# Narrow-tile matmul runs merged and placed side by side, with half of the weighted-value products written over V

## The chip, the cores and the metric

One core of a Trainium2 chip runs the kernel. The metric is the device time of one execution in microseconds (us). "Span" is the time from the first to the last instruction in a profile; it is some 1.7 us shorter than the timed figure in the same execution.

## The reference

```python
xn = _layernorm(x)                       # x: 1 x 2048 x 512, bf16
# A: attention, 32 heads of 16, each row looks at W = 8 rows, 2 apart, backwards
q, k, v = split(xn @ wqkv)
idx = pos[:, None] - arange(8) * 2       # negative ones masked
logits = einsum("bhsd,bhswd->bhsw", q, k[idx]) * Dh ** -0.5
o = einsum("bhsw,bhswd->bhsd", softmax(logits), v[idx])
# B: gated feed-forward, 1376 wide
h = gelu(xn @ w_gate) * (xn @ w_up)
return x + o @ wo + h @ w_down
```

## The kernel before

The rows are worked on in four blocks of 512 (0 to 3). Almost all matmuls are 128 columns of weights by 512 columns of data: Q, K, V (L1130), gate and up (L1367), the output sums (L1442, L1446). Attention over 8 neighbours is not a matmul, so Vector (DVE) multiplies Q by shifted K (the logit products, 8 per block), and TensorE only adds up groups of rows, with weights of ones and zeros. These sums use the array as four tiles of 32 columns side by side (`tile_position`), four matmuls abreast. A "visit" below is an unbroken run of matmuls in narrow tiles between full-width ones; a "slot" is the time from one matmul's start to the next (0.216 us for 512 columns, or for four such matmuls abreast). The small `u10` piece (the last 64 columns of gate and up) uses tiles of 64 and is issued with the logit sum:

```python
for kt in range(4):                       # u10: two 64-column tiles
    for c in range(2):
        e.matmul(PS[64 * c:64 * c + 64, ...], lhsT=Wt[:, kt, 128:192], rhs=xnT[..., 256 * c:256 * c + 256],
                 start=(kt == 0), stop=(kt == 3), tile_position=(0, 64 * c))
for (g, prs) in grp:                      # logit sum: 32 matmuls, 32-column tiles
    for wq in range(2):
        for sj in range(4):
            e.matmul(PS[32 * sj:32 * sj + 32, ...], lhsT=E8[:, ...],
                     rhs=UNI[:, prs[wq].slot, :, sj * 128:(sj + 1) * 128], ..., tile_position=(0, 32 * sj))
```

The weighted-value sum works in the same way on the products of V and the softmax. V comes back from device memory with shifts into four buffers `BS`; Vector multiplies each twice (half 0 and 1), and both products go to one of twelve buffers `UNI`, shared with the logit products:

```python
e.tensor_tensor(out=bass.AP(UNI, ito.slot * 2048, ...), in0=bass.AP(BS, ...), in1=bass.AP(PT, ...), op=ALU.mult)
...
for (dq_, itp, it) in grp:                # PVR_MERGE = 2 of them: 16 matmuls
    for half in range(2):
        for d4 in range(4):
            e.matmul(PS[32 * d4:32 * d4 + 32, ...], lhsT=E4[:, :], rhs=UNI[:, itp[half].slot, d4, :],
                     start=(half == 0), stop=(half == 1), tile_position=(0, 32 * d4))
```

The order on each engine is made at build time by a planner in the kernel: each piece of work is a task with a priority (shifted by a table `SHIFT`), reads and writes of buffers from pools with quotas, and a mode ("c" for the narrow tiles, "f" for full width).

Of the kernel before, what the change touches and what calls it, by code (L numbers as in the profile page):

```python
# [11 lines left out]
    TOL=dict(pe=0.6, act=-0.3, dve=0.0, pool=0.0, sp=0.0),  # L12
    DMA_ISSUE=0.48,
    DMA_FIXED=2.0,
    DMA_BPUS=330e3,
    ACT_SWITCH=1.35,
    PE_SLACK=0.0,
# [128 lines left out]
class Graph:  # L146
# [118 lines left out]
    def schedule(self, params=None, prior=None):  # L265
# [4 lines left out]
        TOL = prm["TOL"]  # L270
        DMA_ISSUE = prm["DMA_ISSUE"]
        DMA_FIXED = prm["DMA_FIXED"]
        DMA_BPUS = prm["DMA_BPUS"]
        ACT_SWITCH = prm["ACT_SWITCH"]
        PE_SLACK = prm["PE_SLACK"]
# [3 lines left out]
        pe_mode = [None]  # L279
# [78 lines left out]
        while nsched < ntot:  # L358
# [43 lines left out]
            for e, cl in cands.items():  # L402
                tol = TOL[e]
                cur = list(cl)
                if prior is not None and use_virtual[0]:
                    pmin = min(c[1].prio for c in cl)
                    real = set(c[1].idx for c in cl)
                    hor = efree[e] + 6.0
                    for t in unsched[e]:
                        if t.start is None and t.idx not in real and t.prio < pmin and t.latest is None:  # L410
                            ps = prior.get(t.idx)
                            if ps is not None and ps < hor:
                                cur.append((max(ps, efree[e]), t, 0.0, ps, True))
                while True:
                    top = min(cur, key=lambda c: (c[1].prio, c[1].idx))
                    lim = top[3] + tol
                    nxt = [c for c in cur if c is not top and
                           c[0] + c[2] + (DMA_ISSUE if e == "sp" else c[1].dur) <=
                           (lim if c[1].latest is None else top[3])]
                    if not nxt:  # L420
                        break
                    cur = nxt
                pick = top
                if pick[4]:
                    blocked.append(e)
                    continue
                if best is None or (pick[0], pick[1].idx) < (best[0], best[1].idx):
                    best = pick
# [6 lines left out]
            for it in t.items:  # L435
                if it.pool is not None and it.slot is None:
                    pool = it.pool
# [175 lines left out]
    def report(self):  # L613
# [11 lines left out]


SHIFT = {
    "acc0": 91, "acc2": 150, "acc3": 165, "er0": -90, "er3": -43, "ffn0": -489, "ffn1": 431, "ffn2": 3,
    "ffn3": 355, "fin2": -301, "fin3": -17, "h1": -471, "h2": -1698, "ldb2": 617, "ln1": -107, "ln2": -2,
    "ln3": -224, "prod1": 434, "prod2": -302, "prod3": -2237, "pv1": 744, "pv3": -110, "pvr0": -321,  # L630
    "pvr1": -1104, "pvr2": -106, "pvr3": 108, "qkv2": 179, "qkv3": -756, "sm2": 1187, "sm3": 124,
}
SCHED = dict(PE_SLACK=1.0, DMA_BPUS=250e3,
             TOL=dict(pe=0.3, act=-0.3, dve=-0.3, pool=-0.3, sp=0.0))

GROUPS = ((r"(?:bnst|bnag|ve|sq|rstd|sub|norm)(\d+)$", "ln", 4), (r"trx(\d+)", "ln", 2),
          (r"(?:mm|evq|evk|evv|stv)(\d)_", "qkv", 1), (r"pr(\d)_", "prod", 1), (r"er(\d)_", "er", 1),
# [21 lines left out]
def d_dve(n, rate=1.04):  # L659
    return 0.07 + n * rate * 1e-3  # L660
# [6 lines left out]
def bass_parallel_sum__sliding_local_dilated__glu_gated_geglu__prompt_kernel(nc, A_x, A_wqkv, A_wo, B_x, B_w_gate, B_w_up, B_w_down, out, dbg=None, cfg=None):  # L667
    cfg = dict(cfg or {})
# [5 lines left out]
    NUNI = cfg.get("NUNI", 12)  # L674
# [7 lines left out]
    NBS = cfg.get("NBS", 4)  # L682
# [3 lines left out]
    NXR = cfg.get("NXR", 2)  # L686
    NOB = cfg.get("NOB", 3)
    NDMASEM = cfg.get("NDMASEM", 24)
    QUOTAS = cfg.get("QUOTAS", dict(tp=2, qkv=2, lg=2, o=cfg.get("PVR_MERGE", 2), ffn=3,
                                    acc=2))  # L690
    PB_ = cfg.get("PRIO_BLOCK", 1000)
    LN_BASE = cfg.get("LN_BASE", [-30, 10, 1010, 2010])
# [1 line left out]
    R_WG = cfg.get("R_WG", -800)  # L694
    TAIL_SPLIT = {14: [(0, 256), (256, 512)], 15: [(0, 256), (256, 384), (384, 512)]}
    NHALF = cfg.get("NHALF", [1, 1, 1, 1])
    PVR_MERGE = cfg.get("PVR_MERGE", 2)
    CHAIN_SHIFT = cfg.get("CHAIN_SHIFT", [0, 300, 600, 900])
    FFN_BASE = cfg.get("FFN_BASE", 500)
    FFN_STEP = cfg.get("FFN_STEP", 1000)  # L700
# [8 lines left out]
    with contextlib.ExitStack() as es:  # L709
# [57 lines left out]
        P_qt = Pool("qt", NQT)  # L767
        P_kt = Pool("kt", 2)
        KTI = [Item("kt%d" % b, P_kt, "k") for b in range(4)]
        P_uni = Pool("uni", NUNI, quotas=cfg.get("UNI_Q", dict(p=8, pv=8)))  # L770
        P_ms = Pool("ms", NMS)
        P_pb = Pool("pb", NPB)
        P_pt = Pool("pt", NPT)
# [283 lines left out]
        for b in range(NB):  # L1057
# [7 lines left out]
            if b == 0:  # L1065
                lead = []
                for t in range(4):
                    for which in range(2):
# [15 lines left out]
                               + ([(XTI[0], ("y", 0, t))] if t < 2 else []))  # L1084
                        gs = (0, 1, 2, 3)
                        if t == 0 and which == 0:
                            t_mm = G.task("pe", "mma0_0", 12 * 0.0563, mk_mm((0, 1, 2)), rd=mrd, wr=[it_mm],
                                          prio=-100, mode="f")
                            t_mm.urgent = True
                            t_of["mma0_0"] = t_mm  # L1090
                            gs = (3,)
                        t_mm = G.task("pe", "mmt%d_%d" % (which, t), 4 * len(gs) * 0.0563, mk_mm(gs), rd=mrd,
                                      wr=[it_mm], prio=-100 + t, mode="f")
                        t_mm.urgent = True
# [82 lines left out]
            for g in range(4):  # L1177
                prs = []
                for wq in range(2):
                    it_pr = pr_items[g][wq]  # L1180
                    prs.append(it_pr)

                    def mk_p(wq=wq, g=g, it=it_pr, itq=it_qt, itk=KTI[b]):
                        return lambda e: e.tensor_tensor(  # L1184
                            out=UNI[:, it.slot, :, :],
                            in0=bass.AP(QT, (itq.slot * 4 + g) * 512, [[NQT * 4 * 512, 128], [0, 4], [1, 512]]),
                            in1=bass.AP(KT, (itk.slot * 4 + g) * 528 + 4 - 2 * wq, [[2 * 4 * 528, 128], [4, 4], [1, 512]]),
                            op=ALU.mult)
                    rdk = ([(KTI[0], ("t", t)) for t in range(4)] if b == 0 else [(KTI[b], g)]) + [(KTI[b], "pad")]
                    rdq = [(it_qt, ("t", t)) for t in range(4)] if b == 0 else [(it_qt, (g, 0))]  # L1190
                    G.task("dve", "pr%d_%d_%d" % (b, wq, g), d_dve(2048, 0.52), mk_p(),
                           rd=rdq + rdk, wr=[(it_pr, "d")] + ([(q, "a") for gg in range(g, g + ER_MERGE) for q in pr_items[gg]
                                                      if q is not it_pr] if g % ER_MERGE == 0 and wq == 0 else []),
                           prio=base + 20)
# [96 lines left out]
                   prio=base + 37, nbytes=256 * 1024)  # L1291

            it_ot = Item("ot%d" % b, P_ot, "ot")
            pv_items = [[Item("pv%d_%d_%d" % (b, dq, half), P_uni, "pv") for half in range(2)] for dq in range(4)]
            pvr_grp = []
            for dq in range(4):
                it_bs = Item("bs%d_%d" % (b, dq), P_bs, "bs")
                for j in (0, 2, 1, 3):
                    def mk_l(j=j, dq=dq, it=it_bs, c0b=c0b):
                        return lambda e: e.dma_start(  # L1300
# [11 lines left out]
                for half in range(2):  # L1312
                    def mk_pv(half=half, it=it_bs, ito=it_pv[half], itp=it_pt):
                        o = 2 - 2 * half
                        return lambda e: e.tensor_tensor(  # L1315
                            out=bass.AP(UNI, ito.slot * 2048,
                                        [[NUNI * 2048, 128], [512, 4], [128, 4], [1, 128]]),
                            in0=bass.AP(BS, it.slot * 4 * 514 + o,
                                        [[NBS * 4 * 514, 128], [514, 4], [128, 4], [1, 128]]),
                            in1=bass.AP(PT, itp.slot * 1024 + half * 128,  # L1320
                                        [[NPT * 1024, 128], [0, 4], [256, 4], [1, 128]]),
                            op=ALU.mult)
                    G.task("dve", "pv%d_%d_%d" % (b, dq, half), d_dve(2048, 0.52), mk_pv(),
                           rd=[it_bs, it_pt], wr=[(it_pv[half], "d")] + ([(q, "a") for dd in range(dq, dq + PVR_MERGE) for q in pv_items[dd]
                                                      if q is not it_pv[half]]
                                                     if dq % PVR_MERGE == 0 and half == 0 else []), prio=base + 50)
                it_o = Item("o%d_%d" % (b, dq), P_ps, "o")
                pvr_grp.append((dq, it_pv, it_o))
                if len(pvr_grp) == PVR_MERGE:
                    def mk_pr(grp=list(pvr_grp)):  # L1330
                        def f(e):
                            ins = None
                            for (dq_, itp, it) in grp:
                                for half in range(2):
                                    for d4 in range(4):
                                        ins = e.matmul(PS[32 * d4:32 * d4 + 32, 512 * it.slot:512 * it.slot + 512],  # L1336
                                                       lhsT=E4[:, :], rhs=UNI[:, itp[half].slot, d4, :],
                                                       start=(half == 0), stop=(half == 1),
                                                       tile_position=(0, 32 * d4))
                            return ins  # L1340
                        return f
                    G.task("pe", "pvr%d_%d" % (b, dq), PVR_MERGE * 0.4315, mk_pr(),
                           rd=[q for g_ in pvr_grp for q in g_[1]] + [I_E4], wr=[g_[2] for g_ in pvr_grp],
                           prio=base + 7, mode="c")
                    for (dq_, itp_, it_) in pvr_grp:
# [77 lines left out]
            for ti in range(4):  # L1423
# [8 lines left out]
                for ci, (c0, c1) in enumerate(cparts):  # L1432
# [39 lines left out]
                    def mk_so(t=t, it=it_ob, c0=c0, c1=c1, CW=CW):  # L1472
                        return lambda e: e.dma_start(out2[128 * t:128 * t + 128, c0:c1], OB[:, it.slot, 0:CW])
                    G.task("sp", "sto" + sfx, 0, mk_so(), rd=[it_ob], wr=[(I_out, (t, ci))], prio=base + 62,
                           nbytes=128 * CW * 2)

        for t in G.tasks:
            t.prio += shift_of(t.name)
        G.schedule(SCHED)
# [51 lines left out]
```

## Time and profile before

| | before |
|---|---|
| time, median (3 runs first, 4 with the result) | 196.65 us; 196.64 us |
| span of the profile | 194.7 us |
| TensorE (PE) busy | 188.9 us, 97% |
| Vector (DVE) busy | 153.8 us, 79% |
| ScalarE (ACT) busy | 104.0 us, 53% |
| visits to narrow tiles | 11 (4 logit sums, 8 half sums, one pair adjacent) |

TensorE is the chain that ends last. Because nothing makes it wait after the first 8 us, its timeline can be cut in three: the start up to the first full-width V matmul, the stretch from there to the start of the last group of matmuls, and 3.3 us of tail. These two lines of TensorE's timeline (columns: start, us, engine, line, operation, count) mark the cuts in the kernel before:

```profile
14.71 3.40 PE L1130 MATMUL PS<-xnT,Wqkv 128*128 128x512 bf16 x15
...
191.42 0.78 PE L1446 MATMUL PS<-Wd,HT 128*128 128x128 bf16 x11
```

The stretch is 191.42 - 14.71 = 176.71 us.

### The profile page before, as it was taken

The page shows a single profiled execution, that of the slowest core. Times are in us where ns is not written, and L with a number is a line of the kernel's source. Part 1 is how long each engine was busy: PE and PEld are TensorE (multiplying, and loading weights), DVE is VectorE, ACT ScalarE, POOL GpSimd, SP SyncE. Part 2 cuts the span into 40 slices and gives each one's busy share as a digit, 9 for nine tenths or more (in the row PEclk, how much of TensorE's full clock was granted, in tenths as well). Part 3 has the DMA queues.
Part 4 walks back from the last instruction along what each step waited for, and adds up shares of the span by engine and source line. Part 5 has one row for each costly group of instructions (what it writes and reads, how often), then busy time and mean ns, then how long its engine had stood idle before and what let it go on. Part 6 is the DMA issues. An engine that isn't in the chain of part 4 may idle for free.

```text
span 194.7 us, 3220 instructions
## 1 busy us (share of the span) xinstructions
PE 188.9 (97%) x1205; PEld 91.0 (47%) x1224; DVE 153.8 (79%) x241; ACT 104.0 (53%) x171; POOL 9.9 (5%) x31
## 2 busy tenths in 40 slices
PE   7999999999999999999999999999999999999994
PEld 2794444444444444444444444444444444344484
DVE  5889998879969899999998956999995619972132
ACT  3487764686896748403377321674779106586000
POOL 6011000102100010000001100000000000000000
DMA  5999995999440847263465652213861340010121
GB/s 130 356 395 302 331 190 124 265 252 211 111 109 0 213 110 194 83 162 109 108 172 153 84 136 71 91 52 92 236 175 46 104 140 27 0 59 0 40 82 40
DMA packets 34799, 27.03 MB, mean 139 GB/s; under 512 B 11264, under 2 KB 33248, under 8 KB 34784
## 3 DMA queue, kind: packets, MB, share of 16 engines
q1 hardware_dynamic: 34784, 26.83, 52.7%
q8 instruction: 9, 0.15, 0.3%
q14 instruction: 6, 0.05, 0.1%
HBM read 19.99 MB, written 5.26 MB: 130 GB/s over the span
## 4 chain that ended last, share of the span: by engine, by line
PE 95%; DMA 2%; issue 1%; SPq 0%; ACT 0%; DVE 0%; DVEq 0%
PE PS L1367 35%; PE PS L1446 20%; PE PS L1130 18%; PE PS L1442 7%; PE PS L1336 4%; PE PS L1214 4%; PE PS L1076 4%; DMA Wqkv<-in_A_wqkv_dram 2%; PE PS L1402 2%; PE PS L1207 1%; SPq L919 0%; PE PS L1018 0%; ACT xnT L1038 0%; DVE OB L1466 0%; DVEq L558 0%
## 5 line engine op out<-in xcount | busy, mean ns | idle before, releaser
L1446 PE MATMUL PS<-Wd,HT 128*128 128x512 bf16 (+2 forms) x206 | 41.0, 345 | 0.2
L1367 PE MATMUL PS<-xnT,Wg 128*128 128x512 bf16 x154 | 39.8, 379 | 0.5 <-issue 0.3
L1367 PE MATMUL PS<-xnT,Wu 128*128 128x512 bf16 x155 | 39.8, 379 | 0.5 <-issue 0.3
L1184 DVE TENSOR_TENSOR UNI<-QT,KT 128x2048 bf16<-128x2048 bf16 x32 | 37.2, 1220 | 1.6 <-ACT KT L1147 1.6
L1315 DVE TENSOR_TENSOR UNI<-BS,PT 128x2048 bf16<-128x2048 bf16 x32 | 37.4, 1218 | 0.7 <-DMA BS<-vt_scratch 0.6
L1384 ACT ACTIVATE UU<-PS 128x512 bf16<-128x512 f32 x40 | 24.0, 601 | 22.2 <-PE PS L1367 22.1
L1130 PE MATMUL PS<-xnT,Wqkv 128*128 128x512 bf16 x156 | 35.1, 379 | 0.3 <-issue 0.2
L1377 ACT ACTIVATE GG<-PS 128x512 bf16<-128x512 f32 x40 | 23.8, 601 | 19.4 <-PE PS L1367 17.6
L1446 PEld LDWEIGHTS PS<-Wd,HT 128*128 128x128 bf16 x209 | 19.6, 98 | 18.5
L1466 DVE TENSOR_TENSOR OB<-PS,XR 128x512 bf16<-128x512 f32 (+2 forms) x19 | 11.4, 600 | 17.9 <-PE PS L1446 17.9
L1367 PEld LDWEIGHTS PS<-xnT,Wg 128*128 128x128 bf16 x160 | 15.2, 98 | 19.8 <-ACT UU L1384 1.3
L1367 PEld LDWEIGHTS PS<-xnT,Wu 128*128 128x128 bf16 x160 | 15.3, 98 | 19.6 <-issue 0.8
L1130 PEld LDWEIGHTS PS<-xnT,Wqkv 128*128 128x128 bf16 x160 | 15.5, 98 | 19.0 <-issue 0.4
L1389 DVE TENSOR_TENSOR HT<-GG,UU 128x512 bf16<-128x512 bf16 x40 | 16.3, 423 | 9.1 <-ACT UU L1384 8.6
L1442 PE MATMUL PS<-Wo,OT 128*128 128x512 bf16 (+2 forms) x75 | 16.7, 345 | 0.0
L1140 ACT ACTIVATE QT<-PS 128x512 bf16<-128x512 f32 x12 | 7.2, 597 | 9.6 <-PE PS L1130 9.6
L1154 ACT ACTIVATE VT<-PS 128x512 bf16<-128x512 f32 x16 | 9.5, 597 | 4.1 <-PE PS L1130 4.1
L936 DVE BATCH_NORM_STATS2 st<-XIN 128x6 f32<-128x512 bf16 x16 | 10.6, 686 | 1.0 <-DMA XIN<-in_A_x_dram 1.0
L1442 PEld LDWEIGHTS PS<-Wo,OT 128*128 128x128 bf16 x76 | 7.2, 98 | 7.0
L1347 ACT ACTIVATE OT<-PS 128x512 bf16<-128x512 f32 x16 | 8.7, 598 | 2.7 <-PE PS L1336 2.7
L1147 ACT ACTIVATE KT<-PS 128x512 bf16<-128x512 f32 x12 | 7.2, 598 | 4.9 <-PE PS L1130 4.9
L1076 PE MATMUL PS<-xnT,Wqkv 128*128 128x128 bf16 x128 | 8.0, 219 | 0.5 <-ACT xnT L1038 0.3
(63 smaller groups left out, 131.9 us busy)
## 6 DMA issues: line engine op xcount, KB each, us to landing
BS<-vt_scratch SPq DMA_DIRECT2D x64, 128.5 KB, 2.7
vt_scratch<-VT SPq DMA_DIRECT2D x16, 128.0 KB
XR<-in_A_x_dram SPq DMA_DIRECT2D x16, 128.0 KB, 2.2
out_dram<-OB SPq DMA_DIRECT2D x14, 128.0 KB, 2.0
Wqkv<-in_A_wqkv_dram SPq DMA_DIRECT2D x3, 512.0 KB, 5.3
XIN<-in_A_x_dram SPq DMA_DIRECT2D x6, 256.0 KB, 5.5
Wg<-in_B_w_gate_dram SPq DMA_DIRECT2D x1, 1280.0 KB
Wu<-in_B_w_up_dram SPq DMA_DIRECT2D x1, 1280.0 KB
```

The source lines that it names most:

```text
L936: return lambda e: e.bn_stats(out=st[:, t, :], in_=XIN[:, it.slot, t2, :])
L1076: ins = e.matmul(PS[:, 512 * it.slot + 128 * g:512 * it.slot + 128 * g + 128], lhsT=Wqkv[:, kt, which * 512 + g * 128:which * 512 + (g + 1 ...
L1130: ins = e.matmul(PS[:, 512 * it.slot:512 * it.slot + HWD], lhsT=lhsT, rhs=xnT[:, itx.slot, kt, c0:c0 + HWD], start=(kt == 0), stop=(kt == 3))
L1184: return lambda e: e.tensor_tensor(out=UNI[:, it.slot, :, :], in0=bass.AP(QT, (itq.slot * 4 + g) * 512, [[NQT * 4 * 512, 128], [0, 4], [1, ...
L1315: return lambda e: e.tensor_tensor(out=bass.AP(UNI, ito.slot * 2048, [[NUNI * 2048, 128], [512, 4], [128, 4], [1, 128]]), in0=bass.AP(BS, ...
L1367: ins = e.matmul(PS[0:M, 512 * it.slot:512 * it.slot + 512], lhsT=Wx[:, kt, j * 128:j * 128 + M], rhs=xnT[:, itx.slot, kt, :], start=(kt = ...
L1377: return lambda e: e.activation(out=GG[0:M, ito.slot, :], in_=PS[0:M, 512 * it.slot:512 * it.slot + 512], func=ACTF.Gelu_apprx_tanh)
L1384: return lambda e: e.activation(out=UU[0:M, ito.slot, :], in_=PS[0:M, 512 * it.slot:512 * it.slot + 512], func=ACTF.Identity)
L1389: return lambda e: e.tensor_tensor(out=HT[0:M, ito.slot, j, :], in0=GG[0:M, ig.slot, :], in1=UU[0:M, iu.slot, :], op=ALU.mult)
L1442: ins = e.matmul(PS[:, 512 * it.slot:512 * it.slot + CW], lhsT=OT[:, ito.slot, dq, ti * 128:(ti + 1) * 128], rhs=Wo[:, dq, c0:c1], start=( ...
L1446: ins = e.matmul(PS[:, 512 * it.slot:512 * it.slot + CW], lhsT=HT[:, ith.slot, j, ti * 128:(ti + 1) * 128], rhs=Wd[:, j, c0:c1], start=Fal ...
L1466: return lambda e: e.tensor_tensor(out=OB[:, ito.slot, 0:CW], in0=PS[:, 512 * it.slot:512 * it.slot + CW], in1=XR[:, itx.slot, c0:c1], op= ...
```

## The change

The intent: let a block's weighted-value sum run directly beside the next block's logit sum, so that TensorE goes into the narrow tiles less often. That needs all eight value products of one block and all eight logit products of the next at the same moment, 16 buffers where UNI has 12. So half of the value products are written in place, over the V that they were made from. Besides, the sums are issued as one run of 32, and Q of the first tile is cut at 8 of 16 matmuls, not 12. The diff, shortened:

```diff
-                    top = min(cur, key=lambda c: (c[1].prio, c[1].idx))
+                    top = min(cur, key=lambda c: (c[1].prio - (1e6 if c[1].mode == "c" == pe_mode[0] else 0), c[1].idx))
...
 SHIFT = { ... all priorities retuned ... }
-SCHED = dict(PE_SLACK=1.0, ..., TOL=dict(..., dve=-0.3, ...))
+SCHED = dict(PE_SLACK=1.6, ..., TOL=dict(..., dve=0.3, ...))
...
-    QUOTAS: o=cfg.get("PVR_MERGE", 2)      PVR_MERGE = cfg.get("PVR_MERGE", 2)
+    QUOTAS: o=4                            PVR_MERGE = cfg.get("PVR_MERGE", 4)
-        UNI_Q: dict(p=8, pv=8)
+        UNI_Q: dict(p=8, pv=4)
...
-   t_mm = G.task("pe", "mma0_0", 12 * 0.0563, mk_mm((0, 1, 2)), ...)
+   t_mm = G.task("pe", "mma0_0", 8 * 0.0563, mk_mm((0, 1)), ...)
...
+                        def dst():
+                            if half == 0:
+                                return bass.AP(UNI, ...)
+                            return bass.AP(BS, ito.slot * 4 * 514, ...)
                         return lambda e: e.tensor_tensor(
-                            out=bass.AP(UNI, ...),
+                            out=dst(),
...
-                       lhsT=E4[:, :], rhs=UNI[:, itp[half].slot, d4, :],
+                       lhsT=E4[:, :], rhs=(UNI, BS)[half][:, itp[half].slot, d4, 0:512],
...
+        for b in range(NB - 1):            # sum b after all logit products of block b + 1
+            ... G.order_after(t_of["pvr%d" % b], t_of["pr%d_%d_%d" % (b + 1, wq, g)])
```

## The prediction

> **What bounds the kernel now.** I read the page's table of engines first, then the shares of the chain of waits that ended last, then TensorE's waits, and last its timeline group by group. Of the page, one line from each of the first two:
>
> ```profile
> PE 188.9 (97%) x1205; PEld 91.0 (47%) x1224; DVE 153.8 (79%) x241; ACT 104.0 (53%) x171; POOL 9.9 (5%) x31
> ...
> PE 95%; DMA 2%; issue 1%; SPq 0%; ACT 0%; DVE 0%; DVEq 0%
> ```
>
> The chain is TensorE (PE) for 95% of the span. "Busy" alone would not prove that, so here are TensorE's waits, the whole answer without its heading:
>
> ```profile
> PE PS L862 <- DVE wsrc L811: 1.2, 1, 1.2
> PE PS L1367 <- issue: 0.6, 4, 0.2
> PE PS L1076 <- ACT xnT L1038: 0.3, 1, 0.3
> PE PS L1076 <- DMA Wqkv<-in_A_wqkv_dram: 0.2, 1, 0.2
> PE PS L1130 <- issue: 0.2, 1, 0.2
> ```
>
> Everything that names another engine here lies in the first 8 us (L862 is the warm-up; L1076 is Q and K of the first block). After that TensorE waits for nobody. The five "issue" waits of 0.16 us are each a matmul record missing behind a logit sum: the row shows 3 or 15 matmuls where 4 or 16 were issued. So the only things that can shorten the span are fewer TensorE slots, cheaper slots, or the start. Slots are read from starts, because the ends are modelled. TensorE's timeline around one weighted-value sum (L1336; columns: start, us, engine, line, operation, count):
>
> ```profile
> 96.58 1.03 PE L1367 MATMUL PS<-xnT,Wu 128*128 128x512 bf16 x4
> 97.54 1.05 PE L1336 MATMUL PS<-UNI,E 128*32 128x512 bf16 x16
> 98.52 1.04 PE L1367 MATMUL PS<-xnT,Wg 128*128 128x512 bf16 x4
> 99.39 1.03 PE L1367 MATMUL PS<-xnT,Wu 128*128 128x512 bf16 x4
> 100.26 1.03 PE L1367 MATMUL PS<-xnT,Wg 128*128 128x512 bf16 x4
> ```
>
> An undisturbed group of four 512-column matmuls takes 0.863 us (99.39 to 100.26), so a matmul 0.2158. The group before the sum takes 0.957 (96.58 to 97.54): +0.093 for going over to 32-column tiles. The 16 matmuls of the sum run four abreast and should take 4 x 0.2158 = 0.863, but take 0.98: +0.117. The group after takes 0.873: +0.010. One visit to the narrow tiles with one sum of 16 therefore wastes 0.22 us. Where a logit sum follows such a sum directly, the same view shows what adjacency saves:
>
> ```profile
> 66.30 1.05 PE L1336 MATMUL PS<-UNI,E 128*32 128x512 bf16 x16
> 67.28 0.63 PE L1207 MATMUL PS<-xnT,Wt 128*64 128x256 bf16 x8
> 67.83 1.91 PE L1214 MATMUL PS<-UNI,E 128*32 128x512 bf16 x32
> ```
>
> The sum still takes 0.98 and the 64-column piece 0.56, but L1207 has no 0.093 in front of it. L1214's 32 matmuls take 1.84 in the chain, that is 8 x 0.2158 + 0.117: the 0.117 is paid once per run of equal narrow matmuls, not per 16.
>
> **What the Trainium skill says.** "TensorEngine Tiling (Array Packing)", Key Properties: changing the tiling mode, not just the tile, drains TensorE. The trace agrees: 0.22 us per visit above. "TensorE: Matmul & The Clock Gate", Back-to-back issue gap, gives N/2.4 + 2.5 ns for a warm isolated matmul, 215.8 ns at N=512, and some 131 ns as a sustained figure; this trace's stream shows the first (0.2158 us), not the second, so no faster slot is to be hoped for. "VectorE: DVE Perf Modes", Mode 2x_1P, wants 16-bit operands, unit step and 4-byte alignment; writing a product over V keeps that (rows of 514 elements), and V is already read at that pitch today in 1.218 us a product, so I expect the in-place products to cost the same. The same page, The DRAIN you can't avoid, says that a semaphore between two Vector operations costs nothing extra. The trace differs: products follow each other every 1.135 us, and the maximum L1247 (72.05), whose reader L1252 waits on it, takes 1.25 to the next start:
>
> ```profile
> 72.05 1.22 DVE L1247 TENSOR_REDUCE ms<-PS 128x128 f32<-128x1024 f32 x1
> 73.30 1.23 DVE L1252 TENSOR_TENSOR PS<-PS,ms 128x1024 f32<-128x1024 f32 x1
> 74.56 0.87 DVE L1417 TENSOR_TENSOR HT<-GG,PS 64x256 bf16<-64x256 bf16 x2
> ```
>
> An equal operation that the next one does not wait for takes 1.13, so I charge 0.125 for a dependent pair.
>
> **The change part by part.** I listed the instruction order of the built kernel, engine by engine, with what each waits for.
>
> (a) Weighted-value sums: before, eight of 16 matmuls; after, four of 32. The 0.117 is paid 4 times instead of 8: -4 x 0.117 = -0.47 us. No matmul is added or removed.
>
> (b) Visits to narrow tiles. Before, there are 11: four logit sums and eight half sums, one pair adjacent. After, the order is: logit sum 0; sum 0 with logit sum 1; sum 1 with logit sum 2; logit sum 3 alone (sum 2 did not join it, in spite of the intent); sum 2 alone; sum 3 alone. That is 6: -5 x (0.093 + 0.010) = -0.52 us.
>
> (c) Q of the first tile, 12 matmuls before the next transpose become 8. TensorE's timeline there:
>
> ```profile
> 6.25 0.83 PE L1076 MATMUL PS<-xnT,Wqkv 128*128 128x128 bf16 x12 [0.23 <-DMA Wqkv<-in_A_wqkv_dram]
> 6.92 0.39 PE L1018 MATMUL PS<-ident,XIN 128*128 128x128 bf16 x4
> 7.14 0.39 PE L1076 MATMUL PS<-xnT,Wqkv 128*128 128x128 bf16 x4
> 7.78 1.12 PE L1076 MATMUL PS<-xnT,Wqkv 128*128 128x128 bf16 x17 [0.25 <-ACT xnT L1038]
> ```
>
> The matmuls at 7.78 wait for ACT's copy of the transpose at 6.92. Eight matmuls end at 6.25 + 8 x 0.056 = 6.70, the normalised input is there at 6.68 (L992 ends) plus about 0.055, so the transpose starts at about 6.73: 0.18 earlier. The copy and the next normalisation follow it, so -0.18 us reaches everything behind, unless the K weights (issued at 2.74, 5.3 to landing: 8.0, needed at 8.5) are later than I read.
>
> (d) Vector products in place: 32 products as before, at 1.135 a step, but the second of each pair now waits for the first. At most 16 x 0.125 = 2 us of Vector time, on an engine busy 79%; it counts only where TensorE then waits.
>
> (e) Waits moved. All eight value products, and the next block's eight logit products (an added order), must be ready before a sum, and V's buffers come free only at the end of the sum, so all 16 loads of the next V start there. I added up Vector's work along each TensorE entry, with TensorE's own clock from its counts x 0.2158 (the same count for before ends within 0.02 us of the trace).
> - Sum 0 with logit sum 1: from the end of logit sum 0 (31.9 in my count) the softmax, two normalisations, eight logit products, the next layer-norm pieces and eight value products with four H products between them end at 70.75; TensorE arrives at 71.7. Slack 0.9 us, the thinnest.
> - Sum 1: the V weights in probabilities (PT) land at about 95.1, because their store and load stand behind output stores on the queue; four pairs of 1.26 + 1.135 end at 104.8; TensorE at 107.1. Slack 2.3.
> - Logit sum 3: after logit sum 2, Vector has maximum 1.26, subtraction 1.14, two products 2.27, H 0.34, sum 1.26, reciprocal 0.98, scaling 1.14, output add 0.60 and four products 4.7 = 13.8 with latency; TensorE has 70 matmuls, 15.2. Slack 1.4. The first two logit products of that block wait only for sum 1, not for logit sum 2; otherwise 2.3 more would make this a stall of 0.9.
> - Sum 2: slack about 1.7. Sum 3: 16 loads of V at 0.475 us an issue plus 2.7 to landing, then products and two output adds, end some 17 us after sum 2; TensorE has 92 matmuls, 19.9. Slack over 2.5.
> - ACT empties four sum banks in 2.2 us while TensorE works 3.4 us or more elsewhere: no wait seen.
>
> Sum: -0.47 - 0.52 - 0.18 = -1.17 us, on 196.65: 195.5. I leave 0.1 for a small wait at one of the thin entries: **195.6 us**.
>
> **The rivals.** (1) Vector becomes late at an entry: the in-place dependency, the added order and the merging all push work in front of one instant. For it: a slack of 0.9 on a count of some 45 Vector instructions, and 79% busy. Against it: four of five entries have over 1.3. If one entry stalls by 0.5 to 1 us, the time is 196.1 to 196.6, and the gain is gone. (2) V's loads: they start as one burst after each sum. Against it: 7.6 us of issue and 2.7 of landing fit in front of every sum; if the last did not, it would be a stall directly before the tail, +1 to +2 us, 196.6 to 197.6. (3) The start gain is hidden: a weight or input transfer lands when it lands, then -0.99 alone, 195.7. (4) The drain at a visit depends on more than the count, for instance on alternating UNI and BS as source inside the merged sum, so that each switch of source costs 0.1: 28 of them would be +2.8 us, 198. Nothing in the trace speaks for that; L1214 changes its source buffer eight times without a cost.
>
> **Range and chances.** The terms (a) and (b) are counts of a measured cost, good to some 0.1; (c) is worth 0 to 0.2; one stall of up to 0.7 us is what I allow above. Low: 195.2. High: 196.3. Faster by over 2% would be under 192.7, which would need TensorE slots that the change does not remove: 0.01. Slower by over 2% is over 200.6, for which several stalls would have to add up: 0.01. Within 2%: 0.98.
>
> **What would show it.** In the changed profile: six visits to narrow tiles, the sums with x32 or its pieces in 1.84 us each; the group before each visit at 0.96; the first full-width V matmul 0.18 earlier; TensorE's waits free of Vector after 8 us; in-place products at 1.22 like the others, with 1.26 between a pair's starts. The prediction is wrong if TensorE waits for a Vector product or a V load at an entry, above all sum 0 or logit sum 3, or if a merged sum takes clearly more than 1.84.

## The result

The changed kernel takes 195.28 us (median of 4 runs, 195.06 to 195.65) against 196.64 of the kernel before in the same rounds. The ratio is 0.9933, with a 95% interval of 0.9916 to 0.995. Ratios are the mean time of one kernel's fast runs over that of the other's of the same rounds, so not quite the ratio of the medians. The prediction was 195.6, range 195.2 to 196.3.

The page's table of engines and the shares of the chain, after:

```profile
PE 187.4 (97%) x1207; PEld 91.6 (47%) x1224; DVE 153.2 (79%) x241; ACT 104.0 (54%) x171; POOL 16.2 (8%) x31
...
PE 93%; ACT 2%; DVE 2%; DMA 1%; issue 1%; DVEq 0%
```

TensorE is as full as before, and by the page busy for 1.5 us less (the ends of its matmuls are modelled; the stretch, read from starts below, lost 0.98); Vector is nearly unchanged. The chain's 2% each of ScalarE and Vector are places where its walk goes over them (1.84 us over ScalarE's copies of sum 2 at 152.62, for instance); they are no waits of TensorE, as its own list shows. TensorE's waits, the whole answer without its heading (columns: who waited for whom, us in total, times, longest):

```profile
PE PS L863 <- DVE wsrc L812: 1.5, 1, 1.5
PE PS L1077 <- DVE rstd L969: 0.7, 1, 0.7
PE PS L1374 <- issue: 0.6, 4, 0.2
PE PS L1131 <- issue: 0.2, 1, 0.2
```

After the start there is again no wait for another engine (the "issue" entries are missing matmul records). The `rstd` named for the first Q matmuls is an inference of the profile: they don't read it. So the gain must be in TensorE's own slots, or in the start. There are six visits to narrow tiles, as listed in the prediction: logit sum 0 at 29.05, the two joint ones at 71.27 and 106.69, logit sum 3 at 126.14, sum 2 at 150.66, sum 3 at 172.47. One joint visit in TensorE's timeline after the change, sum 0 with u10 and logit sum 1:

```profile
71.27 0.40 PE L1342 MATMUL PS<-UNI,E 128*32 128x512 bf16 x4
71.49 0.39 PE L1342 MATMUL PS<-BS,E 128*32 128x512 bf16 x4
...
73.11 0.63 PE L1208 MATMUL PS<-xnT,Wt 128*64 128x256 bf16 x8
73.67 1.91 PE L1215 MATMUL PS<-UNI,E 128*32 128x512 bf16 x32
```

The sum's 32 matmuls take 73.11 - 71.27 = 1.84 us, as a logit sum's 32 do; the switches between UNI and BS come every 0.216 us, the bare slot of four abreast, so they cost nothing. The two marks of the stretch:

```profile
14.49 3.40 PE L1131 MATMUL PS<-xnT,Wqkv 128*128 128x512 bf16 x15
...
190.22 0.78 PE L1453 MATMUL PS<-Wd,HT 128*128 128x128 bf16 x11
```

The stretch is 175.73 us: 0.98 less than 176.71. The start is 0.22 shorter in this pair of profiles, although the warm-up matmuls begin 0.26 later in the changed plan (the waits on `wsrc` are 1.5 and 1.2 us, because Vector clears it second and not first; all profiles of each plan show this); the tail is the same. Vector's timeline at the first in-place product (L1322, half 1 has BS as its output):

```profile
59.97 1.22 DVE L1322 TENSOR_TENSOR UNI<-BS,PT 128x2048 bf16<-128x2048 bf16 x1
61.22 1.22 DVE L1322 TENSOR_TENSOR BS<-BS,PT 128x2048 bf16<-128x2048 bf16 x1
62.37 1.22 DVE L1322 TENSOR_TENSOR UNI<-BS,PT 128x2048 bf16<-128x2048 bf16 x1
```

The in-place product lasts as long as the other; it starts 1.25 us after the product that it must wait for, and the next, which waits for no product, 1.15 after it.

### The profile page after: what moved, and what is told of

The parts are those of the page before. It is cut to its first block, busy times and chain, and to the rows that moved or that the text cites. A ratio compares the mean times of both kernels' runs of the same rounds, so it can differ in the third digit from the quotient of the medians.

```text
span 193.5 us, 3221 instructions
## 1 busy us (share of the span) xinstructions
PE 187.4 (97%) x1207; PEld 91.6 (47%) x1224; DVE 153.2 (79%) x241; ACT 104.0 (54%) x171; POOL 16.2 (8%) x31
## 4 chain that ended last, share of the span: by engine, by line
PE 93%; ACT 2%; DVE 2%; DMA 1%; issue 1%; DVEq 0%
PE PS L1374 34%; PE PS L1453 20%; PE PS L1131 18%; PE PS L1449 7%; PE PS L1077 4%; PE PS L1342 4%; PE PS L1215 4%; PE PS L1409 1%; PE PS L1208 1%; DMA XIN<-in_A_x_dram 1%; ACT OT L1354 1%; DVE st L937 1%; PE PS L1019 0%; ACT UU L1391 0%; DVE XIN L976 0%
## 5 line engine op out<-in xcount | busy, mean ns | idle before, releaser
L1374 PE MATMUL PS<-xnT,Wg 128*128 128x512 bf16 x154 | 39.3, 379 | 0.7 <-issue 0.5
L1473 DVE TENSOR_TENSOR OB<-PS,XR 128x512 bf16<-128x512 f32 (+2 forms) x19 | 11.4, 602 | 11.8 <-PE PS L1453 11.6
L1322 DVE TENSOR_TENSOR UNI<-BS,PT 128x2048 bf16<-128x2048 bf16 x16 | 19.5, 1219 | 0.6 <-DMA PT<-pt_scratch 0.5
L1322 DVE TENSOR_TENSOR BS<-BS,PT 128x2048 bf16<-128x2048 bf16 x16 | 19.6, 1222 | 0.3
L1171 POOL COPY KT<-KT 128x64 bf16<-128x64 bf16 x3 | 7.6, 2518 | 40.0 <-ACT KT L1148 38.6
```

What stands on the lines that cost most here:

```text
L1322: return lambda e: e.tensor_tensor(out=dst(), in0=bass.AP(BS, it.slot * 4 * 514 + o, [[NBS * 4 * 514, 128], [514, 4], [128, 4], [1, 128]]) ...
L1374: ins = e.matmul(PS[0:M, 512 * it.slot:512 * it.slot + 512], lhsT=Wx[:, kt, j * 128:j * 128 + M], rhs=xnT[:, itx.slot, kt, :], start=(kt = ...
L1473: return lambda e: e.tensor_tensor(out=OB[:, ito.slot, 0:CW], in0=PS[:, 512 * it.slot:512 * it.slot + CW], in1=XR[:, itx.slot, c0:c1], op= ...
```

## The experiments

The table gives for each run the start and the stretch, read as above, and what the account of the prediction (0.103 for a visit, 0.117 for a run of equal narrow matmuls, nothing else) makes of the stretch. Those with a plan of their own are marked. The runs: the first (chip 2) is q1_only to u10_in_32, the second (chip 6) the three repeats, the third (chip 6) u10_first and the two "alone" runs. "Before" was 196.32 us in the first and 196.50 in the second; for the runs made once (u10_first, the two "alone" runs and no_pref) that same 196.50.

| run | start | stretch | stretch by the account | time, median |
|---|---|---|---|---|
| before | 14.71 | 176.71 | | 196.64 |
| changed | 14.49 | 175.73 | 175.73 | 195.28 |
| q1_only | 14.56 | 176.71 | 176.71 | 196.38 |
| no_q1 | 14.94 | 175.72 | 175.73 | 195.74 |
| merge_2 (own plan) | 14.69 | 176.39 | 176.39 | 196.06 |
| u10_in_32 | 15.07 | 175.02 | 174.99 | 195.03 |
| changed_rep | 14.69 | 175.72 | 175.73 | 195.35 |
| no_q1_rep | 14.88 | 175.73 | 175.73 | 195.45 |
| u32_rep | 14.68 | 175.02 | 174.99 | 194.67 |
| u10_first | 14.47 | 175.62 | 175.61 | 195.03 (one run) |
| merge_4_alone (own plan) | 14.78 | 178.02 | 175.93 | 197.75 (one run) |
| in_place_alone (own plan) | 14.55 | 178.75 | 176.71 | 198.24 (one run) |
| no_pref (own plan) | 14.47 | 189.27 | 175.94 | 208.69 (one run) |

The theory was that of the prediction: slots saved, in a stretch without waits, plus an earlier start. The rivals: the gain comes from somewhere else (operands, not tile widths), or the start's share isn't real.

### The start: Q cut at 8, alone and undone

Edit of q1_only, on the kernel before (no_q1 is the reverse, on the changed kernel; in both, the planned durations are kept, so that nothing else moves):

```diff
-   t_mm = G.task("pe", "mma0_0", 12 * 0.0563, mk_mm((0, 1, 2)), ...)
+   t_mm = G.task("pe", "mma0_0", 12 * 0.0563, mk_mm((0, 1)), ...)
-   gs = (3,)
+   gs = (2, 3)
```

> The kernel before with nothing but Q's first 12 matmuls cut to 8 (all instructions otherwise in the old order). My account: the second tile's transpose starts 0.21 us earlier and everything behind follows, so the first full-width V matmul starts at 14.50 instead of 14.71 and the time is 196.64 - 0.21 = 196.43 us. Rival (the start's gain is hidden behind a weight or input transfer): V start at 14.50 but a wait later on TensorE, time 196.6 as before.

> The changed kernel with Q's first group put back to 12 matmuls, all else in the same order. My account: +0.21 us, 195.28 + 0.21 = 195.5, first V matmul at 14.71, all visits to narrow tiles unchanged. Rival (the start's gain is hidden): 195.3, as the changed kernel.

q1_only: 196.38 us (6 runs, 196.20 to 198.34) against 196.32, ratio 1.0018 (0.9988 to 1.0048). The expected 0.21 us did not come, although the profiled start was 14.56; without the one run at 198.34, too, the means are equal (196.39). no_q1: 195.74, ratio 0.9973 to the kernel before, some 0.5 us, though its stretch is 0.99 shorter: the rest went in its start (14.94 in the profile). It can't be compared closely with 195.28. It was run at another time. So I repeated it beside the changed kernel itself:

> The changed kernel itself, unedited, on the same chip as the next two: what is disputed is the start. So far TensorE's stretch from the first full-width V matmul to its last matmul was the same to 0.01 us wherever the order was the same (176.713 us in the kernel before and with Q's cut alone; 175.726 us in the changed kernel with and without the cut), while the start in front of it lay between 14.50 and 15.07 us. I expect 175.73 again for the stretch, a start anywhere in 14.4 to 15.1 (two causes: when the first weights land, and when the matmuls go over from 107 to 56 ns each), and a median time of 195.3 to 195.6.

> The same with Q's first group back at 12 matmuls. If the cut is worth its full 0.21 us in every run: median 0.2 us above the one just before. My present account: the cut pays only in runs in which the first weights land so late that 12 matmuls would end after the second tile is normalised (at some 6.7 us); where they land early it pays nothing, so on average about 0.1 to 0.15 us, at the edge of what five rounds show. Stretch 175.73.

changed_rep: 195.35 (5 runs, 195.27 to 195.36), ratio 0.9943. no_q1_rep: 195.45 (6 runs, 195.15 to 195.75), ratio 0.9947. Means 195.34 and 195.44: a difference of 0.1 us, which the scatter of six runs (195.15 to 195.75) tells neither from nothing nor from the 0.18 charged. The profiles show why the worth of the cut is not constant. TensorE's timeline at the start of no_q1_rep:

```profile
6.43 0.83 PE L1077 MATMUL PS<-xnT,Wqkv 128*128 128x128 bf16 x12 [0.78 <-DMA Wqkv<-in_A_wqkv_dram]
7.09 0.39 PE L1019 MATMUL PS<-ident,XIN 128*128 128x128 bf16 x4
```

and of q1_only:

```profile
5.99 0.62 PE L1076 MATMUL PS<-xnT,Wqkv 128*128 128x128 bf16 x8
6.76 0.40 PE L1018 MATMUL PS<-ident,XIN 128*128 128x128 bf16 x4 [0.15 <-DVE XIN L992]
```

In the first, the weights land late (6.43), twelve matmuls end at 6.43 + 12 x 0.056 = 7.10, and the transpose follows at once: eight would have let it start some 0.22 earlier. In the second, the weights land early: twelve matmuls would have ended at about 6.66, before the transpose could start at all, because it waits for Vector until 6.76. The cut pays only when the weights are late against the normalised second tile. Worked out in the same way for all eight profiles with the cut, it saved 0.22 us in the changed kernel, about 0.2 in merge_2, 0.3 in u10_in_32 and at most 0.05 in the other five: an estimate of 0.1 on average. In changed_rep the weights were as late as in the changed kernel (6.26), but the tile was ready at 6.82 instead of 6.56.

A second cause moves the start, and it is larger. In u10_in_32, with the same instructions at the start:

```profile
6.37 1.01 PE L1077 MATMUL PS<-xnT,Wqkv 128*128 128x128 bf16 x8 [0.20 <-ACT sq L951]
7.17 0.50 PE L1019 MATMUL PS<-ident,XIN 128*128 128x128 bf16 x4
```

Eight matmuls take 7.17 - 6.37 = 0.80 us, 0.10 each; in the changed kernel's own profile they take 0.45, 0.056 each. The Trainium skill, "TensorE: Matmul & The Clock Gate", Part 1 (the HAM clock gate), says that TensorE runs at half clock until a free-running window of about 3.4 us has been busy, and that the moment varies from run to run. The traces agree in kind: matmuls go over to the full rate at 4.9 us in the changed kernel and at 7.4 us in u10_in_32, with the first matmul at 1.51 in both; the earliest of all profiles is in_place_alone, at some 4.15 us (the warm-up matmul at 3.78 takes 0.40 us, the one at 4.18 takes 0.22) with the first matmul at 1.25, so 2.9 us after it. The start of u10_in_32 was 15.07 against 14.49.

### The sums in halves again

```diff
-    PVR_MERGE = cfg.get("PVR_MERGE", 4)
+    PVR_MERGE = cfg.get("PVR_MERGE", 2)
```

> The changed kernel with the weighted-value sums issued in halves of 16 again, ordered anew by its planner. The built order has 9 visits to narrow tiles (logit sum 0; half sum + logit sum 1; half; half; half + logit sum 2; logit sum 3; half; half; two halves of block 3 together). My account, counts only: 3 more visits x 0.103 and 7 runs of equal narrow matmuls instead of 4, 3 x 0.117, together +0.66 us: 195.9. Rival: the halves let Vector's products and V's loads flow more evenly, so nothing is lost: 195.3 or less. Second rival: a wait on Vector appears at one entry: 196.5 or more.

Measured 196.06 us (5 runs, 196.02 to 196.28), ratio 0.9988 (0.9977 to 1.0). The stretch is 176.39, so +0.66 on the changed kernel: exactly the three visits and three runs that were counted, 3 x (0.103 + 0.117), and its trace has the 9 visits. TensorE waits for nobody after the start. Both rivals fall: merging neither costs nor hides anything here, and no wait is behind the difference.

### The 64-column piece: what the 0.12 us belongs to

u10_in_32 and its repeat u32_rep:

```diff
-   for c in range(2):
-       ins = e.matmul(PS[64 * c:64 * c + 64, ...], lhsT=Wt[:, kt, 128:192], ..., tile_position=(0, 64 * c))
+   for q in range(4):
+       c, h = q // 2, q % 2
+       ins = e.matmul(PS[32 * q:32 * q + 32, ...], lhsT=Wt[:, kt, 128 + 32 * h:160 + 32 * h], ...,
+                      tile_position=(0, 32 * q))
```

> The changed kernel with the 64-column piece in front of each logit sum cut into 16 matmuls in 32-column tiles (same results, same place, same order), so that no change of tile width is left inside a visit. Theory A (a change of tile width costs some 0.12 us, and four 32-column matmuls of 256 columns run abreast in 0.108 us): -0.127 at logit sums 0 and 3 and -(0.117+0.127) at the two joint visits, together -0.74 us: 194.55; the joint visit shrinks from 4.47 to 4.23 us. Theory B (a narrow matmul can't be issued faster than one per 0.054 us, so cutting the work finer costs): each piece takes 0.86 instead of 0.43, +1.73 in all, less 0.74: +1.0, 196.3. Theory C (the 0.12 belongs to a change of operands, not of tile width): 195.3.

> The changed kernel with the 64-column piece in 32-column tiles, beside the changed kernel itself. The first run of it showed a stretch of 175.016 us, 0.71 less than the changed kernel, as theory A said, but a time only near the changed kernel's, because its matmuls ran at 107 ns until 7.4 us. Expected: stretch 175.02 and a median 0.7 us below the changed kernel of this call, 0.4 to 1.0 with the noise of the start. If the stretch's gain does not reach the time: under 0.2.

The joint visit in u32_rep, behind the sum at 71.33:

```profile
73.07 0.61 PE L1209 MATMUL PS<-xnT,Wt 128*32 128x256 bf16 x16
73.51 1.90 PE L1216 MATMUL PS<-UNI,E 128*32 128x512 bf16 x32
75.57 1.24 PE L1131 MATMUL PS<-xnT,Wqkv 128*128 128x512 bf16 x5 [0.16 <-ACT OT L1355]
```

The sum now takes 73.07 - 71.33 = 1.74 (1.84 before), the piece 0.44 (0.56 before), although it has twice the matmuls: sixteen at 0.027 us each. The time from the first narrow matmul to the next full-width one is 4.24 against 4.47 (each with one missing record behind the logit sum, 0.216 us; the wait on `OT` in the last line is that gap, which the changed kernel's list calls "issue"). The stretch lost 0.71 of the 0.74 expected, in both runs. Theory A holds, B and C fall. In the first call (195.03; 6 runs, 194.71 to 196.88) there was no changed kernel to compare with; against no_q1 of the same call, which has the changed kernel's stretch, the median is 0.71 lower, despite one run at 196.88. Beside the changed kernel it is there again: 194.67 (4 runs, 194.44 to 194.83), ratio 0.9908 (0.9895 to 0.9922), so means 194.65 against 195.34, -0.68 us. This is the best version, 1.8 us under the kernel before, with correct results.

u10_first moves the 64-column piece to the front of one joint visit, keeping its width (edit in short):

```diff
+   for t, n in zip(pe_o, pe_o[1:]):             # after planning, before the waits are set
+       if t.name.startswith("pvr") and n.name == "er1_3":
+           t.deps |= n.deps - {t}
+           t.emit = lambda e: (u10(e), sum0(e))   # and logit sum 1 without its u10
```

> The changed kernel with the 64-column piece of logit sum 1 moved in front of sum 0, in the same visit, so that sum 0 (32 matmuls with one set of weights) and logit sum 1 (32 with another) stand next to each other in 32-column tiles; all else in place. Theory A (the cost is per change of tile width): one change fewer, -0.12 us in that visit (4.25 to 4.13 from its first start to the next full-width matmul) and in the stretch, 175.61. Theory C (the cost is per run of equal matmuls, whatever the width): unchanged, 175.73.

That visit in TensorE's timeline:

```profile
71.25 0.63 PE L1208 MATMUL PS<-xnT,Wt 128*64 128x256 bf16 x8
...
73.32 0.39 PE L1350 MATMUL PS<-BS,E 128*32 128x512 bf16 x4
73.54 1.90 PE L1223 MATMUL PS<-UNI,E 128*32 128x512 bf16 x32
```

The last four of the sum take 73.54 - 73.32 = 0.22, the bare slot: going from one set of weights to another at the same width costs nothing. The stretch is 175.62, one change of width less, as theory A said (175.61). The move was made in this one joint visit. In the other, logit sum 2's task waits in the plan for ScalarE to empty a bank (`GG`, 107.04 to 107.64 in the changed kernel), which is after the visit begins (106.69), so moving it forward would cost a wait; no run shows it.

### The parts of the change alone

merge_4_alone is the kernel before with `PVR_MERGE` 4; in_place_alone is the kernel before with half 1 written over BS; no_pref is the changed kernel with the first line of the diff undone.

> The kernel before with the weighted-value sums merged to 32 matmuls and nothing else (no product in place, no preference, old priorities), planned anew. Built order: logit sum 0; logit sum 1; sum 0; logit sum 2; sum 1; logit sum 3; sum 2; sum 3: 8 visits, none joined. By counts alone: -3 x 0.103 - 4 x 0.117 = -0.78 us, 195.7. My account: twelve product buffers can't hold eight value products and eight logit products, so sum 0 now comes after logit sum 1 and each sum's eight products queue for buffers that the other sum frees; somewhere behind, TensorE waits on Vector, 2 to 6 us in all: 198 to 202.

> The kernel before with half of the value products written in place over V and nothing else (sums still in halves of 16), planned anew; 11 visits as before, one of them joined. If writing in place is neutral by itself: 196.5. My account: V's four buffers now come free at the end of a sum, not of a product, so the next V loads start later and Vector gets its V late; with the old priorities that reaches TensorE: 1 to 4 us, 197.5 to 200.5, with a wait on a value product.

> The changed kernel without the planner's preference for staying in the narrow tiles, planned anew: sum 0 and logit sum 1 come apart (logit sum 1 now 80 full-width matmuls later), so do sum 1 and logit sum 2: 8 visits. If the visits alone matter: 2 x 0.103 = +0.2, 195.5. My account: the late logit sum 1 pushes the later blocks' softmax and sums behind it until TensorE runs out of other work in the last third; the planner's own estimate for this order is 24 us longer, of which I believe most: 212 to 222 us, with waits on Vector or ACT before the last sums.

All three are slower than the kernel before (one run each, state unknown: 197.75, 198.24, 208.69), and the first is also just under its expected 198 to 202. merge_4_alone saves its slots and loses 178.02 - 175.93 = 2.09 us to waits. They are not the direct wait on Vector that I expected. TensorE's largest wait on another engine there, from its list of waits (`GG` is the gelu of a gate result):

```profile
PE PS L1367 <- ACT GG L1377: 1.3, 1, 1.3
```

The same place in ScalarE's timeline (ACT):

```profile
151.01 1.28 ACT L1259 ACT_TABLE_LOAD   x1
152.98 1.01 ACT L1259 ACTIVATE PS<-PS 128x1024 f32<-128x1024 f32 x1 [0.68 <-DVE PS L1252]
154.00 1.28 ACT L1377 ACT_TABLE_LOAD   x1
155.30 0.60 ACT L1377 ACTIVATE GG<-PS 128x512 bf16<-128x512 f32 x1
```

ScalarE stands ready for the softmax's exponential, which waits for Vector's subtraction, and empties no gate bank for 4.3 us; then TensorE has no bank to write. in_place_alone has its main wait, 1.7 us, also on a bank that `GG` empties, but at another place: the output products at 180.85. ScalarE had stood idle 2.4 us for the last half sum (178.11), and copies its banks out before it turns to the gate bank. That half sum itself had waited only 0.2 on an in-place product. So in-place writing does not slow Vector's products, but in the old plan it is not free either. That the V loads start later is what I would blame; the runs don't show it, and the cause stays open.

no_pref has waits of the kind that I expected, but fewer of them (209 us, not 212 to 222). From TensorE's list of waits:

```profile
PE PS L1342 <- DVE BS L1322: 7.0, 2, 6.8
PE PS L1449 <- ACT OT L1354: 4.6, 2, 2.4
```

Without the preference, logit sum 1 comes some 90 full-width slots (19.7 us) behind sum 0, and the blocks behind it follow. At sum 2 TensorE waits 6.8 us for a value product, and twice more it waits over 2 us for a sum's result to be copied out. After the wait of 6.8 us, sum 2's matmuls come every 0.43 us four abreast, not 0.216 (32 matmuls, so 1.7 us more; the mean granted clock of this run was 0.984, 1.0 elsewhere). With the waits (11.6 us) that makes up the 13.3 us lost. The preference is therefore worth far more than two visits (0.2 us): without it this table of priorities is a bad plan.

## Why the prediction was right

- **What bounds it, and the slots.** Terms (a) and (b), 0.99 us together, came out as 0.98 in the stretch. merge_2 took back 0.66 of them by the same two prices. One thing in the account was not right: it charged the 0.117 to each run of equal narrow matmuls. u10_in_32 and u10_first show that it belongs to a change of tile width: two runs with different weights but the same width, side by side, pay it once. For the changed kernel both ways of counting give the same sum. A slip of reading had no effect either: of the five "issue" waits, four are behind logit sums and one is behind the last half sum (171.07, 16 matmuls in 1.21 us).
- **No new wait.** The slacks of step (e) held. From the profile, the last product's end and TensorE's arrival are 70.3 and 71.3 at sum 0 (1.0 us; predicted 0.9), 104.5 and 106.7 at sum 1 (2.2; 2.3), 124.9 and 126.1 at logit sum 3 (1.2; 1.4), 148.7 and 150.7 at sum 2 (2.0; 1.7), 168.63 and 172.47 at sum 3 (3.8; over 2.5). The allowance of 0.1 for a small wait was not needed.
- **In place (d).** The pair's step is 1.25 us (charged 1.26), and the duration unchanged at 1.22.
- **The start (c).** The mechanism works in some runs: 0.18 was charged and the profiled pair shows 0.22, but the repeat shows 0.1, which is not told from nothing. Rival (3), which said that a transfer lands when it lands, came out the other way round: the cut is hidden where the weights land early. The prediction did not count the later warm-up of the new plan; no run shows what that costs.
- **What stays open.** The median fell by 1.36 in the first rounds and by 1.15 in the repeat; 1.05 was predicted. The stretch accounts for 0.98 in both. The rest is the start, whose scatter of some 0.6 us (14.47 to 15.07; weights' landing, clock) no count of mine predicts. So it is luck that the first median lay 0.3 under the prediction: 14.49 is one of the earliest starts.
- **Rival (4)**, a cost for alternating UNI and BS, falls: 0.216 us a switch, the bare slot. Rivals (1) and (2) did not occur in the changed plan; no_pref shows that rival (1) is real where the plan is worse.

## What to carry to other kernels

When TensorE never waits, count its changes of tile width and price each from starts in the trace. Then take away the changes themselves, for instance by cutting a 64-column piece into 32-column tiles, which gave another 0.7 us here. Judge effects under 0.5 us by the stretch of the bounding engine between two marks in the trace, because the start of a kernel scatters by as much from run to run. Merging and writing in place paid here with the new priorities: with the old ones, either alone was slower than nothing (one run each). The new priorities without writing in place were not run, so what they would gain by themselves is not shown.

## What the Trainium skill lacked or had wrong

- "TensorEngine Tiling (Array Packing)", Key Properties, says that a mode switch drains TensorE, but gives no price. Here: 0.093 us from 128 to 32 columns, 0.12 to 0.13 at 64 to 32, 0.117 behind a run of 32-column matmuls before another width, and nothing (0.22 for four, the bare slot) for new weights at the same width.
- The same page does not say that finer tiles can be the better choice for a piece between others: 16 matmuls of 32 x 256 took 0.44 us, 8 of 64 x 256 took 0.56 with the switch.
- "TensorE: Matmul & The Clock Gate", Part 1, puts the transition at some 4 us, give or take 0.5. In these runs it came 2.9 (in_place_alone) to 5.9 us after the first matmul, and where it came last, eight matmuls of the start took 0.80 us, not 0.45, and the start ended at 15.07 us, not 14.49.
- "VectorE: DVE Perf Modes", The DRAIN you can't avoid, says of a row of copies that a semaphore between two Vector operations costs nothing extra, but also that a next operation that isn't held starts earlier; it gives no size for that. Here a product that waits for the one before starts 1.25 us after it, one that doesn't 1.14.
